# New places for the work of the first attention layer in a four-layer kernel on one core

## The chip, the core and the metric

The kernel runs on one core of a Trainium2 chip. Its time is device microseconds from start to end of the program, and the number shown is the median of several runs. The core has five engines that run side by side, each with its own queue of instructions: TensorE (PE, with its weight loads listed as PEld), VectorE (DVE), ScalarE (ACT), GpSimd (POOL) and SyncE (SP, which issues nearly all of the DMAs here).

## What is computed

The input x is 2048 x 640 in float32. Four layers follow each other, an attention layer A and a Fourier layer B in turn, each with a residual connection and a layer norm ahead of it:

```python
x = x + _A_ref(_layernorm(x), A_wqkv, A_wo)
x = x + _B_ref(_layernorm(x), dft_seq_re, dft_seq_im, dft_hid_re, dft_hid_im)
x = x + _A_ref(_layernorm(x), A_wqkv, A_wo)
x = x + _B_ref(_layernorm(x), dft_seq_re, dft_seq_im, dft_hid_re, dft_hid_im)
```

Layer A has 32 heads of 20 elements. Each position attends to 8 positions only: itself and those 2, 4, ... 14 places before it. So queries, keys and values come from one matrix product (640 x 1920), and so does the output (640 x 640), but the logits and the weighted sum of the values are elementwise products and sums over short windows:

```python
logits = einsum("bhsd,bhswd->bhsw", q, kg) * scale   # kg: 8 keys for each position
attn = softmax(where(mask, logits, -1e9))
o = einsum("bhsw,bhswd->bhsd", attn, vg)
```

Layer B is Real(DFT over the sequence of DFT over the hidden dimension): two products with 640 x 640 matrices and two with 2048 x 2048 matrices, of which symmetry leaves a part to be computed.

## The kernel before

**Precision.** Every matrix operand is split into a high part (a rounding copy, mostly by ACT) and a low part (the original less the high part, a subtract by DVE or POOL), and each product is three matmul passes: high x high, high x low, low x high. The subtract is called a low part below. It is made by `split` (L137, for weights `wq_split`), `wo_lo` (L584, output weights), `ln_lo` (L918, the normalised output of the layer), `c_lo` (L972, sequence matrix) and `pre_lo` (L956, the part of the sequence matrix that is split early and stored to DRAM as c0b). The high parts are `wo_hi` (L581), `c_hi` (L944) and `pre_hi` (L952).

**Attention.** The sequence is cut into 4 chunks (c) of 512 positions, the columns into 4 groups (q) of 480. 64 QKV groups of 15 matmuls each (`qkv_mm`, L369) write a bank; ACT copies it out (`qkv_evac`, L376); after every second group two DMAs store keys with values (kvb) and queries (qb) to DRAM (L385, L386). Windows of keys and values come back by DMA (`w_load`, L424), queries by `q_load` (L408) and a copy to PSUM by ACT (`q_copy`, L411).

The elementwise work has 32 units u of two halves each, 64 halves in all. For a half, DVE multiplies queries with windows of keys (`qk_mul`, L438, 128 x 1280 elements); POOL adds the upper ten elements of each head to the lower ten (L441); DVE sums the remaining ten (`qk_red`, L448). For the halves listed in `WHOLE` POOL's add is left out, and DVE sums all twenty. The softmax of a unit follows on DVE (L463 to L473) with the exponential on ACT (L456); then DVE multiplies with the values (`av_mul`, L478), and POOL adds the eight products in a tree of three adds (`av_tree`, L497, L498, L499). For the very last half DVE does this sum (L494). Then PE transposes the sums (`pc_pe`, L334, L342), and `wo_mm` (L522) multiplies with the output weights; DVE adds the residual (`wo_add`, L166), statistics and the norm of the next layer follow (`wo_stats`, `wo_fin`, `ln_hi` L914, `ln_lo` L918).

**The next layer's first product inside this one.** The sequence product of layer B (`z_mm`, L985) starts before the attention layer is done: 16 row blocks z, each in three thirds of five 128x512 matmuls, accumulating over z in five banks. Blocks 0 to 9 take a matrix that was split ahead (`pre_load` L948, `pre_hi`, `pre_lo`, `pre_store` L959; fetched by `c_get`), blocks 10 to 12 are loaded and split in place (`c_load`, `c_hi`, `c_lo`), the rest after the attention's end. Block z needs the normalised rows (c, j) with 4c + j = z, high and low part.

**What sets the order.** All of it is written out by hand. `at(step, phase, function, ...)` enters a call into a plan; the steps run from -7 to 66, in each the phases come in the order of `PHASES` (L851 and after), and the calls are emitted in that order inside a manual schedule. Each engine runs its instructions in the order emitted, and waits where data or a buffer isn't ready. Half s = 2u + jp of the elementwise work stands at step s (product), s + 1 (sum), s + 3 (values and tree). QKV group g stands at the step in `LEAD0` for the first 16 groups and then at one group a step, two at the even steps in `TWICE`. SP issues DMAs in this order too; a store stands right behind the instruction that makes its data, and all behind it in SP's queue wait with it.

A rest of the layer follows the last step: the last two rows of chunk 3 (transposes, output projection, norm) and blocks 13 to 15 of the sequence product.

## Time and profile before

| | us |
|---|---|
| median of 3 runs | 1759.59 |
| lowest, highest | 1754.35, 1760.87 |
| the profiled execution | 1757.63 |
| its span in the trace | 1755.8 |
| first attention layer in it, to the release of PE by POOL's last tree | 369.96 |

The profile is one execution. Its slices divide the span into 40 parts of 43.9 us, and a digit is the busy share in tenths. A row of a window view gives a stretch, its length, and for PE, PEld, DVE, ACT and POOL the busy time with the count of instructions; then the granted clock of PE, the DMA share and GB/s. A row of the timeline gives start and duration in microseconds, engine, line, operation, output and inputs by the program's names, shapes and count; a bracket at its end is the idle time of the engine before it, and what ended that. A row of the chain of waits gives start, duration, and what was worked on by the chain that ended last.

### The profile page before, as it was taken

To read this page: it belongs to the slowest core of one execution; us is meant where nothing else is said; L and a number is where in the kernel's file an instruction comes from. 1 tells how busy PE (TensorE), PEld (TensorE's weight loads), DVE (VectorE), ACT (ScalarE), POOL (GpSimd) and SP (SyncE) were. 2 spreads that over 40 slices of the span, in tenths; PEclk is the share of its full clock that TensorE was granted. 3 is DMA by queue.
4 is the path that set the end of the run, shared out by engine and by line. 5 is a ranking of instruction groups with operands and counts; after the bars stand their busy time and mean duration, and the time that the engine had idled before them with its cause. 6 is when DMAs were issued, how large, how long until landed. Compare 5 with 4: busy or idle time off the path is not lost.

```text
span 1755.8 us, 26454 instructions
## 1 busy us (share of the span) xinstructions
PE 1725.6 (98%) x8798; PEld 1501.8 (86%) x8798; DVE 1374.0 (78%) x2131; ACT 805.0 (46%) x1682; POOL 621.2 (35%) x585
## 2 busy tenths in 40 slices
PE   9999999989999999999999999999999999999999
PEld 7889897878888888888898899988788888888888
DVE  6999999988667767767648999989777677676673
ACT  4664544554444445445534434444434443443441
POOL 4799998940000000000028998889200000000000
PEclk9999999999999999999999999999999999999999
DMA  8996769859787787787657866798597868767861
GB/s 286 304 329 206 230 197 333 269 175 303 258 265 245 239 263 238 234 276 225 195 178 238 266 207 211 221 327 277 197 318 251 260 206 265 249 214 235 261 206 53
DMA packets 273961, 426.20 MB, mean 243 GB/s; under 512 B 22656, under 2 KB 153728, under 8 KB 273568
## 3 DMA queue, kind: packets, MB, share of 16 engines
q1 hardware_dynamic: 270624, 422.54, 73.8%
q10 hardware_dynamic: 3200, 1.97, 0.4%
q8 instruction: 70, 1.15, 0.3%
q14 instruction: 67, 0.55, 0.1%
HBM read 339.28 MB, written 85.14 MB: 242 GB/s over the span
## 4 chain that ended last, share of the span: by engine, by line
PE 75%; DVE 11%; DMA 7%; POOL 3%; issue 3%; ACT 1%; SPq 0%; DVEq 0%; ACTq 0%; POOLq 0%
PE m L369 21%; PE aux L1067 13%; PE t L1164 10%; PE m L1164 9%; PE pq L1164 5%; PE xt L1164 5%; PE aux L522 4%; DMA win<-cs_in 3%; PE m L985 2%; PE t L985 2%; DVE pr L478 2%; DVE pr L438 1%; PE xt L985 1%; POOL pr L497 1%; DMA win<-kvb 1%
## 5 line engine op out<-in xcount | busy, mean ns | idle before, releaser
L369 PE MATMUL m<-r,s 128*128 128x480 f32 x1920 | 435.8, 381 | 1.2 <-DVE r L649 0.5
L369 PEld LDWEIGHTS m<-r,s 128*128 128x128 f32 x1920 | 355.1, 188 | 54.9 <-DVE r L652 1.0
L1067 PE MATMUL aux<-r2a,zo 128*128 128x320 f32 x768 | 226.1, 309 | 0.0
L1157 ACT CAST r<-win 128x512 fp32r<-128x512 f32 x246 | 149.6, 620 | 163.6 <-DVE win L1193 90.1
L497 POOL TENSOR_TENSOR pr<-pr 128x640 f32<-128x640 f32 x126 | 205.3, 1629 | 32.6 <-DVE pr L478 32.1
L1067 PE MATMUL aux<-pr,zo 128*128 128x320 f32 x704 | 207.8, 309 | 0.0
L181 POOL TENSOR_TENSOR stats<-stats,mhalf 128x1 f32<-128x1 f32 (+1 forms) x40 | 30.0, 750 | 492.7 <-ACT stats L177 483.7
L438 DVE TENSOR_TENSOR pr<-pq,win 128x1280 f32<-128x1280 f32 x128 | 189.7, 1483 | 11.9 <-DMA win<-kvb 6.6
L1158 DVE TENSOR_TENSOR r<-win,r 128x512 fp32r<-128x512 f32 x246 | 165.4, 687 | 42.8 <-ACT r L1157 41.6
L478 DVE TENSOR_TENSOR pr<-pq,win 128x1280 f32<-128x1280 f32 x128 | 190.7, 1491 | 5.1
L441 POOL TENSOR_TENSOR pr<-pr 128x640 f32<-128x640 f32 x116 | 166.4, 1434 | 17.0 <-DVE pr L438 14.1
L1164 PE MATMUL m<-r,r 128*128 128x512 f32 x594 | 151.0, 389 | 0.0
L1067 PEld LDWEIGHTS aux<-r2a,zo 128*128 128x128 f32 x768 | 144.1, 188 | 1.9
L1164 PE MATMUL t<-r,r 128*128 128x512 f32 x498 | 133.8, 390 | 1.0 <-DVE r L1158 1.0
L1067 PEld LDWEIGHTS aux<-pr,zo 128*128 128x128 f32 x704 | 132.2, 188 | 2.1
L1164 PEld LDWEIGHTS m<-r,r 128*128 128x128 f32 x594 | 111.3, 188 | 22.9
L985 PE MATMUL m<-s,r 128*128 128x512 f32 x384 | 119.5, 399 | 7.5 <-DMA s<-c0b 3.4
L448 DVE TENSOR_REDUCE lg<-pr 128x64 f32<-128x640 f32 (+1 forms) x128 | 112.1, 876 | 8.8 <-POOL pr L441 8.3
L985 PE MATMUL t<-s,r 128*128 128x512 f32 x384 | 117.8, 394 | 0.2 <-DVE ot L1042 0.2
L498 POOL TENSOR_TENSOR pr<-pr 128x320 f32<-128x320 f32 x126 | 112.0, 889 | 9.9
L1164 PEld LDWEIGHTS t<-r,r 128*128 128x128 f32 x498 | 93.4, 188 | 21.4 <-DVE r L1158 1.4
L376 ACT COPY stg<-m 128x480 f32<-128x480 f32 x128 | 70.8, 554 | 81.7 <-PE m L369 61.5
(299 smaller groups left out, 3200.1 us busy)
## 6 DMA issues: line engine op xcount, KB each, us to landing
win<-cs_in SPq DMA_DIRECT2D x351, 256.0 KB, 3.8
r<-xc SPq DMA_DIRECT2D x240, 256.0 KB, 4.3
win<-kvb SPq DMA_DIRECT2D x96, 440.0 KB, 4.3
xa<-cs_in SPq DMA_DIRECT2D x121, 256.0 KB, 3.8
win<-kvb SPq DMA_DIRECT2D x64, 360.0 KB, 4.7
kvb<-stg SPq DMA_DIRECT2D x60, 320.0 KB, 5.3
xc<-stg SPq DMA_DIRECT2D x32, 512.0 KB, 4.2
s<-c0b SPq DMA_DIRECT2D x26, 512.0 KB, 6.2
```

Source lines behind the costliest of these rows:

```text
L369: nc.tensor.matmul(mt[g][:, : 3 * F], st[:, a, k], wq[q][:, b, k], start=n == 0, stop=n == 14)
L438: nc.vector.tensor_tensor(pr, q, wview(u, jp, 0, [[1, FE]]), op=ALU.mult)
L441: nc.gpsimd.tensor_tensor(pv[:, :, 0:10], pv[:, :, 0:10], pv[:, :, 10:20], op=ALU.add)
L448: nc.vector.tensor_reduce(lgs[u][:, :, 2 * jp : 2 * jp + 2].rearrange("p h j w -> p (j w) h"), prq.pop((u, jp)), axis=AX.X, op=ALU.add,)
L478: nc.vector.tensor_tensor(pr.rearrange("p j w (h d) -> p j w h d", d=DH), lgs[u][:, :, 2 * jp : 2 * jp + 2].rearrange("p h j w -> p j w h" ...
L497: g.tensor_tensor(pr[:, :, 0:4], pr[:, :, 0:4], pr[:, :, 4:8], op=ALU.add)
L498: g.tensor_tensor(pr[:, :, 0:2], pr[:, :, 0:2], pr[:, :, 2:4], op=ALU.add)
L985: self.last = nc.tensor.matmul(self.z[t][k], self.xn[c][:, a, j, k * P : (k + 1) * P], self.ct[s][:, b], start=s == 0 and i == 0, stop=s = ...
L1067: self.last = nc.tensor.matmul(self.ym[e][:, :320], zt[(k, a, ri)][:, j2 * P : (j2 + 1) * P], w[:, e * 320 : (e + 1) * 320], start=(k, a, ...
L1157: nc.scalar.copy(hi, raw)
L1158: nc.vector.tensor_tensor(lo, raw, hi.bitcast(F32), op=ALU.subtract)
L1164: nc.tensor.matmul(bank, w(a, kb), hl[b], start=start and (a, b) == (0, 0), stop=stop and (a, b) == (1, 0),)
```

## The change

Only the first attention layer's plan differs; the constants for the second one are written in another form and give the same plan.

- `LEAD0`: QKV groups 5 and 6 stand at step 0 instead of -2 and -1, together with group 7. Their order on PE is the same; their evictions on ACT and group 5's stores come later.
- `TWICE`: second groups at step 13 and 20 instead of 14 and 18.
- `WHOLE`: halves 45, 49, 51 and 59 get POOL's add back, halves 14, 39 and 52 lose it.
- `WQP`: weight low parts (1,2), (2,2) and (3,4) go from DVE to POOL, (2,3) and (3,1) from POOL to DVE.
- `PRD`, `PRV`, `PRP`: of the early split of the sequence matrix, the high parts of blocks 2 and 3 go from DVE to ACT and that of block 7 from ACT to DVE; the low part of block 1 goes to POOL; most stores come one step earlier, low part 2 comes to step 1, low part 3 to step 3.
- `WOR`, `WOS`, `WOP`: output weights are loaded at steps 10, 11 and 14, split at 11 to 17, and low parts 1 and 4 go from DVE to POOL.
- `LNV`: normalised low parts (1,2) and (2,0) go from POOL to DVE, (3,1) from DVE to POOL, behind the last tree.
- `ZT`: each third of the sequence product has a step and a phase of its own. Block 0 and two thirds of block 1 stand at 49, block 2 ahead of the transposes of step 52, two thirds of block 4 at 54, the rest of 4 and two of 5 at 55, block 8 mostly at 60, block 9 at 61 and 62, block 12 at 64. The loads, high and low parts of blocks 4 to 12 move with them; c_lo(10) stands at 61, c_lo(12) at 63.
- `W3`: the output projections of rows (3,0) and (3,1) stand at 61 and 63 instead of 60 and 61, with what follows them.

```diff
@@ -35,22 +35,19 @@
 NE = 8
 FE = 80
 HE = 4
-LEAD0 = (-7, -6, -5, -4, -3, -2, -1, 0, 1, 1, 2, 3, 3, 4, 5, 5)
+LEAD0 = (-7, -6, -5, -4, -3, 0, 0, 0, 1, 1, 2, 3, 3, 4, 5, 5)
 
 
 QJ1 = ((0, 0), (1, 0), (2, 0), (0, 1), (1, 1), (3, 0), (2, 1), (3, 1))
-TWICE = ((8, 10, 12, 14, 16, 18), (10, 14, 18, 20))
+TWICE = ((8, 10, 12, 13, 16, 20), (10, 14, 18, 20))
 OUTP = (((20, 24, 28, 32), (36, 40, 44, 46)), ((20, 24, 28, 32), (36, 40, 44, 46)))
 LNS = ((40, 52), (42, 52))
 
 
 LEAD2 = (-7, -6, -5, -4, -2, -1, 0, 0, 1, 1, 2, 3, 3, 4, 5, 5)
 WSTEP = (0, 0, 0, 1, 1, 2, 2, 3, 3, 4, 4, 5, 5, 6, 7)
-WHOLE = ((43, 45, 47, 49, 51, 55, 57, 59, 63), (51, 57, 63))
-ZTHIRDS = (
-    {49: 3, 50: 3, 51: 2, 52: 4, 56: 3, 57: 6, 58: 3, 59: 4, 60: 2, 61: 1, 62: 3, 63: 4, 64: 1},
-    {50: 3, 51: 5, 52: 1, 53: 1, 54: 1, 55: 1, 56: 5, 57: 4, 58: 3, 59: 3, 60: 1, 61: 1, 62: 4, 63: 2, 64: 4},
-)
+WHOLE = ((14, 39, 43, 47, 52, 55, 57, 63), (51, 57, 63))
+ZT = (((49, 'pe2'), (49, 'pe2'), (49, 'pe2'), (49, 'pe2'), (49, 'pe3w'), (50, 'pe3'), (51, 'pe'), (51, 'pe'), (51, 'pe'), (52, 'pe'), (52, 'pe'), (52, 'pe'), (54, 'pe3'), (54, 'pe3'), (55, 'pe3'), (55, 'pe3'), (55, 'pe3'), (56, 'pe3'), (57, 'pe3'), (58, 'pe3'), (58, 'pe3'), (58, 'pe3'), (59, 'pe3'), (59, 'pe3'), (60, 'peL'), (60, 'pe3'), (60, 'pe3'), (61, 'pe3'), (61, 'pe3'), (62, 'pe3'), (62, 'pe3'), (62, 'pe3'), (62, 'pe3'), (62, 'pe3'), (63, 'pe3'), (64, 'pe3'), (64, 'pe3'), (64, 'pe3'), (64, 'pe3')),
...
 TA = 65
 NWARM = 18
 STG = (-1, "dma2")
@@ -59,9 +56,19 @@
 NT = 8
 NP = 8
 NPAIR = 3
+CLO = (11, 12)
+WQP = (((0, 1), (0, 2), (0, 4), (1, 1), (1, 2), (1, 3), (2, 1), (2, 2), (3, 3), (3, 4)), ((0, 1), (0, 3), (1, 1), (1, 3), (2, 1), (2, 3), (3, 1), (3, 3)))
+LNV = (((1, 2), (2, 0), (2, 1), (2, 3), (3, 0), (3, 2), (3, 3)), ((3, 0), (3, 1), (3, 2), (3, 3), (2, 0), (2, 1), (2, 2), (2, 3), (0, 0), (0, 2)))
+PRD = ((3, 3, 3), (1, 2, 2), (1, 1, 1), (2, 3, 3), (1, 2, 2), (1, 2, 2), (1, 2, 2), (1, 2, 3), (1, 2, 2), (1, 2, 3))
+PRV = (0, 1, 7)
+PRP = (1,)
+WOP = (1, 4)
+WOS = (11, 13, 14, 16, 17)
+WOR = (10, 11, 14)
+W2 = ((52, 53, 54, 55), (52, 53, 54, 55))
+W3 = ((61, 63), (60, 61))
 KEEP = ((10, 11), (12, 13), (14, 15))
-PRE = {4: ("zo2", 0), 5: ("zo3", 2), 6: ("ot", 3), 7: ("zo2", 5), 8: ("zo3", 7), 9: ("ot", 8)}
-PRE.update({0: ('zo0', -5), 1: ('zo1', -4), 2: ('zo0', 0), 3: ('zo1', 0)})
+PRE = {4: ('zo2', 0), 5: ('zo3', 2), 6: ('ot', 3), 7: ('zo2', 5), 8: ('zo3', 7), 9: ('ot', 8), 0: ('zo0', -5), 1: ('zo1', -4), 2: ('zo0', 0), 3: ('zo1', 0)}
 XC = {
     5: ((0, 0), (2, 0), 1),
     7: ((2, 0), (2, 1), -1),
@@ -562,7 +569,7 @@
                     wq[(q, k)] = raw[:, k - k0]
 
         def wq_split(q, k):
-            split(wq[q][:, 0, k], wq[q][:, 1, k], wq[(q, k)], eng=nc.gpsimd if k % 2 else None)
+            split(wq[q][:, 0, k], wq[q][:, 1, k], wq[(q, k)], eng=nc.gpsimd if (q, k) in WQP[ly] else None)
 
         def wq_late(q, k):
             if k == 0:
@@ -581,7 +588,7 @@
             nc.scalar.copy(wo_s["w"][:, 0, k], wo_s[k // 2][:, k % 2])
 
         def wo_lo(k):
-            nc.vector.tensor_tensor(
+            (nc.gpsimd if k in WOP else nc.vector).tensor_tensor(
                 wo_s["w"][:, 1, k], wo_s[k // 2][:, k % 2], wo_s["w"][:, 0, k].bitcast(F32), op=ALU.subtract
             )
             nc.sync.dma_start(wob[:, :, k], wo_s["w"][:, :, k].bitcast(F32))
@@ -697,11 +704,11 @@
         sm = pq[:, o + NJ * HE : o + 2 * NJ * HE].rearrange("p (h j) -> p h j", j=NJ)
         mk = pq[:, o + 2 * NJ * HE : o + 2 * NJ * HE + SLOTS]
         for i in range(3 if first else 0):
-            at(10 + 2 * i, "dma", wo_raw, i)
+            at(WOR[i], "dma", wo_raw, i)
         for k in range(KD):
             if first:
-                at(12 + 2 * (k // 2) + k % 2, "actl", wo_hi, k)
-                at(13 + 2 * (k // 2) + k % 2, "misc", wo_lo, k)
+                at(WOS[k], "actl", wo_hi, k)
+                at(WOS[k] + 1, "misc", wo_lo, k)
             else:
                 at(8 + 2 * k, "dmas", wo_get, k)
 
@@ -790,8 +797,8 @@
                 at(t, "actl", handoff.ln_hi, c, j, nstats)
                 at(t + 1, "misc", handoff.ln_lo, c, j)
         for c, w, xtags in (
-            (2, (52, 53, 54, 55), None),
-            (3, (60, 61), ("xa", "xa")),
+            (2, W2[ly], None),
+            (3, W3[ly], ("xa", "xa")),
         ):
             for j in range(NJ):
                 if c == 2:
@@ -825,11 +832,11 @@
                 at(j2 - 3, "pe3", prev.ymm, NT - 1, j2, 0, KD)
                 at(j2 - 2, "actl", prev.yout, NT - 1, j2, stats)
         last = 66
-        thirds = [t for t, n in ZTHIRDS[ly].items() for _ in range(n)]
+        thirds = [t for t, _ in ZT[ly]]
         for z, (tag, t) in PRE.items() if first else ():
-            d = (2, 2, 3) if z < NJ else (1, 2, 3)
+            d = PRD[z]
             at(t, "dma", handoff.pre_load, z, tag)
-            at(t + d[0], "misc" if z < NJ else "actl", handoff.pre_hi, z)
+            at(t + d[0], "misc" if z in PRV else "actl", handoff.pre_hi, z)
             at(t + d[1], "misc", handoff.pre_lo, z)
             at(t + d[2], "dmac", handoff.pre_store, z)
         for z in range(len(thirds) // 3):
@@ -839,11 +846,11 @@
             elif first:
                 at(t - 2, "dmac", handoff.c_load, z)
                 at(t - 1, "hi", handoff.c_hi, z)
-                at(t - 1, "misc", handoff.c_lo, z, z in (11, 12))
+                at(t - 1, "misc", handoff.c_lo, z, z in CLO)
             else:
                 at(min(t - 1, 48 + z) if z < 3 else t - 1, "dmac", handoff.c_get, z)
             for p in range(3):
-                at(thirds[3 * z + p], "pe" if first and thirds[3 * z + p] == 52 else "pe2" if thirds[3 * z + p] == 52 else "pe3", handoff.z_mm, z, p)
+                at(*ZT[ly][3 * z + p], handoff.z_mm, z, p)
         if first:
             at(62, "dmac", handoff.c_load, 13)
             at(63, "hi", handoff.c_hi, 13)
@@ -914,7 +921,7 @@
             nc.scalar.copy(self.xn[c][:, 0, j], self.xl[(c, j)])
 
         def ln_lo(self, c, j):
-            on_vector = c == NC - 1 or c == 2 and (j % 2 or self.li == 3) or self.li == 3 and c == 0 and j % 2 == 0
+            on_vector = (c, j) in LNV[self.li // 2]
             (nc.vector if on_vector else nc.gpsimd).tensor_tensor(
                 self.xn[c][:, 1, j], self.xl[(c, j)], self.xn[c][:, 0, j].bitcast(F32), op=ALU.subtract
             )
@@ -948,12 +955,12 @@
             nc.sync.dma_start(self.raw[s][:, 1], cs[0][:, s, :])
 
         def pre_hi(self, s):
-            copy = nc.vector.tensor_copy if s < NJ else nc.scalar.copy
+            copy = nc.vector.tensor_copy if s in PRV else nc.scalar.copy
             copy(self.raw[s][:, 0].bitcast(F32R), self.raw[s][:, 1])
 
         def pre_lo(self, s):
             hi, lo = self.raw[s][:, 0], self.raw[s][:, 1]
-            nc.vector.tensor_tensor(lo.bitcast(F32R), lo, hi, op=ALU.subtract)
+            (nc.gpsimd if s in PRP else nc.vector).tensor_tensor(lo.bitcast(F32R), lo, hi, op=ALU.subtract)
 
         def pre_store(self, s):
             nc.sync.dma_start(c0b[:, s], self.raw.pop(s))
```

1 line of the change is left out of this document (added).

## Prediction

> **What bounds the kernel now.** I read the page from its top: busy shares, then the 40 slices, then the shares of the chain that ended last.
>
> ```profile
> span 1755.8 us, 26454 instructions
> PE 1725.6 (98%) x8798; PEld 1501.8 (86%) x8798; DVE 1374.0 (78%) x2131; ACT 805.0 (46%) x1682; POOL 621.2 (35%) x585
> ...
> DVE  6999999988667767767648999989777677676673
> ...
> POOL 4799998940000000000028998889200000000000
> ```
>
> TensorE (PE) is busy for 98% of the span, and the change takes no matmul away. So all that can be won is idle time of PE, in the one stage that is edited: the first attention layer, slices 0 to 8, where VectorE (DVE) and GpSimd (POOL) are full as well. I cut that layer at the places where PE starts and stops waiting. The columns are the stretch, its length, and busy time of PE, weight load, DVE, ACT and POOL.
>
> ```profile
> 0.00:54.00 54.00, 51.67 (x233) 40.60 (x234) 36.77 (x73) 27.12 (x57) 20.94 (x28) 1.00 0.83 281
> 54.00:74.00 20.00, 19.32 (x97) 16.15 (x96) 18.16 (x27) 12.90 (x31) 18.18 (x18) 1.00 1.02 348
> 74.00:270.00 196.00, 196.00 (x1024) 174.35 (x1023) 187.80 (x266) 105.53 (x265) 185.41 (x173) 1.00 0.78 244
> 270.00:316.00 46.00, 41.31 (x238) 36.42 (x237) 44.03 (x69) 20.79 (x55) 40.58 (x39) 1.00 0.98 343
> 316.00:370.00 54.00, 48.75 (x239) 40.42 (x237) 52.24 (x69) 26.08 (x62) 49.85 (x46) 0.97 0.70 228
> 370.00:389.00 19.00, 18.54 (x92) 16.10 (x92) 11.73 (x25) 12.15 (x28) 1.10 (x2) 0.91 0.47 160
> ```
>
> From 74 to 270 us (steps 8 to 47) PE has no gap: nothing that DVE or POOL does there can shorten it. From 270 to 370 PE idles 46.00 - 41.31 + 54.00 - 48.75 = 9.9 us, while DVE idles 3.7 us of the 100. There DVE and POOL set the pace and PE waits. The chain of waits at the end of the layer says which of the two.
>
> ```profile
> 346.34 1.50 DVE pr L478
> ...
> 347.91 1.59 POOL pr L497
> ...
> 366.83 1.54 POOL pr L497
> ...
> 369.38 0.54 POOL zo L499
> 369.96 0.89 PE pq L334 x4
> ```
>
> Up to 347.8 us DVE's value product L478 releases POOL; from 347.91 POOL runs its trees, adds and low parts without a gap, and PE transposes the last tree's sum at 369.96. I call this T. After T the stretch 370 to 389 is PE's own again (18.54 of 19.00). So the kernel gets shorter by as much as T comes earlier, if PE's own queue is not late at T. At most that is the 9.9 us plus the 0.7 us of 54 to 74.
>
> **The change part by part.** The terms are the start, DVE's work in the middle, DVE's work after 270, and POOL's and PE's places.
>
> *Start.* The first query product waits for a window, and the window's load stands in SyncE's queue behind a store of the pre-split sequence matrix (c0b) and a load that needs its place.
>
> ```profile
> 33.27 4.54 DMA c0b<-zo
> 37.83 0.33 SPq L948
> 38.21 4.92 DMA win<-kvb
> 43.22 1.49 DVE pr L438
> ```
>
> With QKV group 5 moved from step -2 to step 0 its two stores no longer stand ahead of the c0b store, and that store is itself moved to step -2. I estimate that the window is loaded some 2 us earlier. DVE also loses two copies of 0.43 us (L952, rows below) at step 2, and gets one at step 6; two pre-split subtracts go to steps 1 and 3, and one to POOL at step -2. DVE is therefore about 1.4 us earlier at step 4. But PE is nearly full there, and what it can give back is its idle time of 54 to 74, 20.00 - 19.32 = 0.7 us. I count **-0.7**. Against it: groups 5, 6 and 7 are still in the same order on PE, but group 7 writes the bank that group 5's eviction frees, and that eviction now stands on ACT behind the first query copy (L411) and four high-part casts of weights. The trace has no such wait; the nearest rows are that copy (0.44 us) and a window's landing (4.92 us), so the place is worth 0 to +4.9. I take 0: the copy is the row of the very operation, and a landing counts only if the query's load is late too. The upper end goes into the range.
>
> *Middle (74 to 270).* The durations by line and shape (count | busy, mean ns | idle before, releaser):
>
> ```profile
> L448 DVE TENSOR_REDUCE lg<-pr 128x64 f32<-128x640 f32 x55 | 44.7, 813 | 5.5 <-POOL pr L441 5.2
> L448 DVE TENSOR_REDUCE lg<-pr 128x64 f32<-128x1280 f32 x9 | 13.3, 1480 | 0.0
> L584 DVE TENSOR_TENSOR r2a<-zo,r2a 128x640 fp32r<-128x640 f32 x4 | 4.8, 1192 | 0.0
> L584 DVE TENSOR_TENSOR r2a<-ot,r2a 128x640 fp32r<-128x640 f32 x1 | 0.8, 812 | 0.0
> L952 DVE CAST zo<-zo 128x512 fp32r<-128x512 f32 x4 | 1.7, 424 | 1.0 <-DMA zo<-cs_in 0.9
> L918 DVE TENSOR_TENSOR r<-xa,r 128x640 fp32r<-128x640 f32 x2 | 1.7, 832 | 0.0
> L441 POOL TENSOR_TENSOR pr<-pr 128x640 f32<-128x640 f32 x55 | 78.9, 1435 | 8.1 <-DVE pr L438 5.3 <-DMA zo<-cs_in 2.6
> L918 POOL TENSOR_TENSOR r<-r,r 128x640 fp32r<-128x640 f32 x6 | 9.4, 1569 | 0.0
> ```
>
> A half that DVE sums whole costs DVE 1.48 - 0.81 = 0.67 us more and spares POOL an add of 1.43. Here halves 14 and 39 become whole: DVE +1.34, POOL -2.9. Two of the five output-weight subtracts (wo_lo, L584) go to POOL, one of the first four and the last (from tile ot): DVE -1.19 - 0.81 = -2.0, POOL +2 x 1.57 = +3.1 (L918 on POOL, the same width). Net: DVE -0.7, POOL +0.2. PE hides it while it lasts, but at 270 DVE takes over, and then it is 0.7 us further on: **-0.7**. The moved output-weight loads and casts, and the weight subtracts exchanged between the two engines (one more on POOL, 0.65 us off DVE), fall into ACT's and POOL's slack of this time; 0.
>
> *After 270.* Halves 45, 49, 51 and 59 go back to POOL and 52 becomes whole: DVE -3 x 0.67 = -2.0, POOL +3 x 1.43 = +4.3. Two normalised low parts, (1,2) and (2,0), come to DVE: +1.66; (3,1), 0.83, leaves it, for POOL after its last tree. DVE: -2.0 + 0.8 = **-1.2**. Is there room on POOL? Its waits for DVE, in order:
>
> ```profile
> 260.31 1.58 POOL L497 TENSOR_TENSOR pr<-pr 128x640 f32<-128x640 f32 x1 [1.22 <-DVE pr L478]
> 280.43 1.58 POOL L497 TENSOR_TENSOR pr<-pr 128x640 f32<-128x640 f32 x1 [1.35 <-DVE pr L478]
> 290.71 1.57 POOL L497 TENSOR_TENSOR pr<-pr 128x640 f32<-128x640 f32 x1 [2.02 <-DVE pr L478]
> 347.91 1.58 POOL L497 TENSOR_TENSOR pr<-pr 128x640 f32<-128x640 f32 x1 [2.34 <-DVE pr L478]
> ```
>
> The four waits, 6.9 us, stand just behind the halves that get their adds back (45, 49, 51, 59), and four adds are 5.7 us. So they are hidden, with 1.2 us left, to which two low parts of 1.57 us that POOL loses come. If that cover is gone, each add costs up to 1.43.
>
> A DVE subtract of two arrays can meet a running POOL instruction. Then both are longer:
>
> ```profile
> 338.64 2.04 DVE L918 TENSOR_TENSOR r<-r,r 128x640 fp32r<-128x640 f32 x1
> 340.60 2.06 DVE L972 TENSOR_TENSOR s<-stg,s 128x512 fp32r<-128x512 f32 x1
> ...
> 339.94 2.17 POOL L497 TENSOR_TENSOR pr<-pr 128x640 f32<-128x640 f32 x1
> ```
>
> 2.04 against 0.83 on DVE, and 2.17 against 1.58 on POOL. The two added low parts may each meet one: 0 to +1.2 each. The split of c_lo(10), now one step after its neighbour, may meet one less: 0 to -1.2. I let these cancel.
>
> [...]
>
> *PE's places.* The sequence product's thirds (L985), the last output projections (L522) and their loads move by one to five steps. Three rows of PE from the end of the layer:
>
> ```profile
> 359.18 0.73 PE L985 MATMUL m<-s,r 128*128 128x512 f32 x2 [2.03 <-POOL s L972]
> 369.96 0.88 PE L334 MATMUL pq<-ident,zo 128*128 128x128 f32 x4 [1.81 <-POOL zo L499]
> ...
> 378.62 0.63 PE L985 MATMUL m<-s,r 128*128 128x512 f32 x2
> ```
>
> PE waits 1.81 us for T; so PE's places cost nothing as long as they are no later by that much, and gain nothing, for T waits on POOL. A split c_lo(12) one step later is followed by its thirds, one step later too. If they fill no gap, PE comes late at T by what is lost: the 2.03 us of the first row again, less the 1.81, about +0.2. The low part (3,1), put on POOL behind the last tree, ends at T + 1.6; the product that reads it cannot start before 378.62, T + 8.7. Loads and stores moved with these steps keep their order of need on SyncE's queue.
>
> **Sum**: -0.7 - 0.7 - 1.2 = -2.6 us. The profiled execution took 1757.63 us (span 1755.8, and 1.8 around it), which makes 1755.0; that execution is 2.0 below the median of the runs shown (1759.59; 1754.35 to 1760.87). Against the median the forecast is **1757.0**.
>
> **The rivals.**
>
> *Fuller gain.* DVE's waits for POOL's adds and others within the layer go too: 5.2 us for L441 (row of L448 above, 8 waits), part of them at the halves 14 and 39 themselves. With 4.3 of them saved: -6.9, **1752.7**. For it: POOL is relieved at steps 14 and 39, and half 39 has the longest of them.
>
> ```profile
> 231.33 0.82 DVE L448 TENSOR_REDUCE lg<-pr 128x64 f32<-128x640 f32 x1 [1.08 <-POOL pr L441]
> ```
>
> Against it: between them POOL gets the two wo_lo, and PE is full until 270.
>
> *No gain.* PE's 196.00 us without a gap also sets when DVE gets its data, since query copies stand behind PE's evictions on ACT, and what is won after 270 is given back where PE comes late (c_lo(12), low part (3,0), each a step later): 0, **1759.6**.
>
> *Moving to POOL helps nothing.* DVE's low parts of wo, moved to POOL, stretch what they meet there: the -2.0 goes, and +1.34 of the middle stays, so -0.7 + 1.3 - 1.2 = -0.6, **1759.0**. For it: the lengthened rows at 338 to 342. Against: the first four L584 were lengthened where they were (mean 1.19 against the last one's 0.81), and a POOL subtract is no DVE instruction that meets anything.
> [...]
>
> *Slower: POOL becomes the bound before 347.9.* Place: POOL's queue between the low part of wo at step 18 and half 59. It gets 3.1 (wo_lo) + 4 x 1.43, loses 3 x 1.43 and two low parts (3.1): +1.4. If each of the two added DVE low parts meets a POOL instruction, 2 x 0.6 on POOL and 2 x 1.2 on DVE come on top: +5.0, and none of DVE's savings counts: **1764.6**. It decides from the point where adds and stretches at 45 to 59 exceed the 6.9 us of waits: 5.7 + 1.2 is just that. Against it: POOL has two low parts less from 316 on.
>
> **How the numbers follow.** About 0.5% (8.8 us) is what a measurement of this kernel tells from no change. Chances: the forecast 0.44, fuller gain 0.16, no gain 0.10, moving helps nothing 0.08, POOL the bound 0.22. The fuller gain stands at -6.9; with the start's 1.4 instead of 0.7, a relieved meeting (1.2) and the weight subtract (0.65) it passes -8.8, for 0.11 of its 0.16. POOL's rival stands at +5.0, and passes +8.8 with the late group 7 (+4.9) on top: 0.13 of its 0.22. So faster 0.11, same 0.76, slower 0.13. The range reaches from the fuller gain, 1752.7 less 3.7 (these three terms, 2.55, and one more meeting of 1.2), to POOL's rival with a little of group 7: 1749 to 1766.
>
> **What would show it.** In the changed profile: the first query product at about 41 us instead of 43.2; PE without a gap from 74 to 270, and the same length of that stretch; the wait of 1.08 at half 39 gone; POOL's waits for L478 behind halves 45, 49, 51 and 59 under 1 us; DVE's busy time between 270 and T about 1.2 us less; T 2 to 3 us earlier, with PE waiting there; 19 us from T to the layer's end. I am wrong if DVE waits for POOL between 120 and 350 us for more than the 5.2 us now (then POOL is the bound), if PE does not wait at T (then PE's places are), if T moves and the end does not, or if the three later layers, which the change leaves alone, move by more than 1 us.

## The result, and the profile after

The changed kernel takes 1750.51 us (median of 20 runs, 1747.03 to 1757.43) against 1755.93 us of the kernel before in the same session (20 runs, 1751.63 to 1761.02): ratio 0.9969, interval 0.9957 to 0.9981, which is 3.3 to 7.6 us less. The forecast was 2.6 us less, 1757.0 us with a range of 1749 to 1766. Sign and range were right; the forecast's size, 2.6 us, is smaller than the interval's lower end. Of the 6.5 us between 1757.0 and 1750.51, 3.7 come from the base: the forecast stood on the 1759.59 us of three runs of the kernel before, and twenty give 1755.93.

The profiled execution took 1755.72 us. Its page, and the windows with the cuts of before (stretch, length, busy time of PE, weight load, DVE, ACT, POOL, then PE's clock):

```profile
span 1753.9 us, 26453 instructions
...
PE 1724.9 (98%) x8798; PEld 1502.2 (86%) x8798; DVE 1372.8 (78%) x2127; ACT 804.9 (46%) x1683; POOL 627.9 (36%) x589
```

```profile
0.00:54.00 54.00, 52.21 (x233) 40.74 (x234) 37.33 (x70) 28.98 (x61) 26.77 (x32) 1.00 0.85 295
54.00:74.00 20.00, 20.00 (x102) 17.43 (x101) 19.52 (x26) 12.73 (x31) 16.91 (x16) 1.00 0.97 328
74.00:270.00 196.00, 194.83 (x1014) 172.63 (x1013) 186.98 (x266) 104.45 (x262) 185.53 (x174) 1.00 0.77 243
270.00:316.00 46.00, 41.73 (x232) 37.00 (x231) 41.65 (x66) 20.55 (x55) 40.82 (x39) 0.96 0.93 333
316.00:370.00 54.00, 49.51 (x251) 42.03 (x249) 51.75 (x72) 26.73 (x64) 50.90 (x47) 0.97 0.69 229
370.00:389.00 19.00, 18.36 (x94) 15.74 (x94) 13.92 (x28) 13.38 (x31) 1.42 (x3) 1.00 0.63 217
```

PE's 0.7 us of idle time at 54 to 74 is gone. In the middle, which had none, there are now 1.2 us of it: waits of 0.43 us at 80.05, 0.20 at 132.86 and 0.54 at 141.88. In this execution DVE has 2.9 us less to do from 270 to 370 (93.4 against 96.3); in a second one of the same kernel it is 96.8, so that this figure doesn't carry. At the end of the layer the timeline of the changed kernel (line numbers are 7 higher there: L506 is the last add of the tree, L341 the transposes, L529 the output projection, L992 the sequence product) reads:

```profile
366.45 2.90 PE L529 MATMUL aux<-r2a,zo 128*128 128x320 f32 x18 [0.19 <-ACT zo L364]
369.19 0.60 PE L341 MATMUL pq<-ident,zo 128*128 128x128 f32 x4
...
377.06 0.63 PE L992 MATMUL m<-s,r 128*128 128x512 f32 x2
...
368.21 0.54 POOL L506 TENSOR_TENSOR zo<-pr 128x160 f32<-128x160 f32 x1
```

POOL's last tree ends at 368.75 instead of 369.91, and PE, which waited 1.81 us for it before, comes to the transposes just behind it and waits for nothing. The product goes on at 377.06 instead of 378.62. So this execution wins 1.6 us in the first layer, and 1.9 at the end of the span. The remainder of the measured 3.3 to 7.6 us isn't in these two traces; the experiments come back to it.

### The profile page after: what moved, and what is told of

It is laid out like the page before. It is cut to its first block, busy times and chain, and to the rows that moved or that the text cites. A ratio compares the mean times of both kernels' runs of the same rounds, so it can differ in the third digit from the quotient of the medians.

```text
span 1753.9 us, 26453 instructions
## 1 busy us (share of the span) xinstructions
PE 1724.9 (98%) x8798; PEld 1502.2 (86%) x8798; DVE 1372.8 (78%) x2127; ACT 804.9 (46%) x1683; POOL 627.9 (36%) x589
## 4 chain that ended last, share of the span: by engine, by line
PE 72%; DVE 11%; DMA 8%; POOL 4%; issue 3%; ACT 1%; SPq 0%; DVEq 0%; ACTq 0%; POOLq 0%
PE m L376 17%; PE aux L1074 14%; PE t L1171 10%; PE m L1171 10%; PE pq L1171 5%; PE xt L1171 5%; PE aux L529 5%; PE m L992 2%; DMA win<-kvb 2%; PE t L992 2%; DVE pr L445 2%; DVE pr L485 2%; DMA xc<-stg 1%; POOL pr L504 1%; DMA win<-cs_in 1%
## 5 line engine op out<-in xcount | busy, mean ns | idle before, releaser
L504 POOL TENSOR_TENSOR pr<-pr 128x640 f32<-128x640 f32 x126 | 207.0, 1643 | 33.9 <-DVE pr L485 33.8
L448 POOL TENSOR_TENSOR pr<-pr 128x640 f32<-128x640 f32 x117 | 168.5, 1440 | 14.7 <-DVE pr L445 11.8
L992 PE MATMUL m<-s,r 128*128 128x512 f32 x384 | 120.1, 400 | 8.3 <-DMA s<-c0b 5.5
L992 PE MATMUL t<-s,r 128*128 128x512 f32 x384 | 118.1, 396 | 0.2 <-DVE ot L1049 0.2
L383 ACT COPY stg<-m 128x480 f32<-128x480 f32 x128 | 71.0, 555 | 84.4 <-PE m L376 63.4
```

Of the source, the lines that this page charges most:

```text
L448: nc.gpsimd.tensor_tensor(pv[:, :, 0:10], pv[:, :, 0:10], pv[:, :, 10:20], op=ALU.add)
L504: g.tensor_tensor(pr[:, :, 0:4], pr[:, :, 0:4], pr[:, :, 4:8], op=ALU.add)
L992: self.last = nc.tensor.matmul(self.z[t][k], self.xn[c][:, a, j, k * P : (k + 1) * P], self.ct[s][:, b], start=s == 0 and i == 0, stop=s = ...
```

## The experiments

Kernels whose parts are undone use the changed file with the constants of before, which gives each engine the same instructions in the same order as the kernel before. The same readings serve all: POOL's last tree (its end, T), the start of PE's 500th and 1900th matmul, counted from 0 in each trace (the 1900th lies in the rest of the layer, at 386.12 us before), and the stretch from the start of DVE's product of half 46 (261.54 us before) to the end of the last tree. That stretch holds the late part of the change but for its first edit, at half 45, and leaves out what a kernel won or lost ahead of it.

| kernel | 500th, against before | half 46 to last tree | last tree ends | 1900th starts | whole time, ratio to before (interval) |
|---|---|---|---|---|---|
| before | 0 | 108.37 | 369.91 | 386.12 | |
| before_again | -0.51 | 108.43 | 369.79 | 386.11 | |
| changed | -0.83 | 107.60 | 368.75 | 384.56 | 0.9969 (0.9957 to 0.9981) |
| again | -0.08 | 105.84 | 367.95 | 383.71 | 0.9966 (0.9945 to 0.9987) |
| p_start | -1.37 | 108.35 | 368.98 | 384.38 | 0.9976 (0.9959 to 0.9993) |
| s_lead | -0.80 | 108.34 | 369.05 | 384.43 | |
| p_mid | +0.95 | 108.39 | 371.67 | 387.06 | 1.0000 (0.9983 to 1.0018) |
| p_late | +1.17 | 106.07 | 368.60 | 384.43 | 0.9983 (0.9968 to 0.9998) |
| l_pe | +0.32 | 107.75 | 369.88 | 385.75 | |
| l_dve | +0.47 | 108.71 | 370.40 | 385.48 | |
| u_wo4 | -1.48 | 110.35 | 370.72 | 386.58 | |
| u_cget | +0.07 | 106.39 | 368.14 | 383.89 | 0.9982 (0.9967 to 0.9996) |
| best2 | -0.42 | 108.68 | 369.98 | 385.73 | 0.9977 (0.9964 to 0.9990) |
| best3 | -1.07 | 105.19 | 366.30 | 382.05 | 0.9973 (0.9961 to 0.9986) |

**How far one trace can be trusted.**

before_again is the kernel before without an edit.

> The kernel before once more, for a second profile. Theory 1 (the first layer repeats, the later layers scatter): PE leaves the first layer (its 1900th matmul) within 0.8 us of the first profile's 386.1 us, the waits of 1.66 us at 275 and of 0.73 at 137 are there again, and the end differs by up to some 8 us for reasons after 500 us. Theory 2 (the first layer itself scatters by several us, so that its -1.6 to -2.4 us in the profiles is chance): 2 us or more off at the 1900th matmul.

Its single run took 1754.9 us. The first layer repeats: last tree and 1900th matmul within 0.12 us, though the 500th came 0.51 us earlier. The two spans differ by 2.8 us (1755.8 and 1753.0), all of it after the layer. Theory 1 holds for this pair: the wait of 0.73 us at 137 is there again (0.75). The 1.66 us at 275 stand in neither timeline as one wait; PE waits 0.43 us at 275.86 in the first and 0.83 at 271.83 in the second.

again is the changed kernel without an edit.

> The changed kernel once more, for a second profile and a ratio of its own. The first profile of it took 1755.7 us, 5.2 above the median of its 20 runs, and shows PE waiting 2.74 us for block 3 of the sequence matrix (DMA, at 291.7 us) with slow matmuls behind it. Theory 1 (an odd landing in that execution): the new profile takes 1748 to 1751 us, that wait is under 1 us, and the layer's end comes 3 to 5 us earlier than in the first. Theory 2 (the wait belongs to the kernel): the wait is again 2 us or more and the layer ends within 1 us of the first profile's; the 5 us lie in later layers. Ratio to before 0.996 to 0.998 by both.

It took 1753.89 us (median), 1756.1 in its profile. Theory 1 is right on the wait and wrong on its price: the wait for block 3 is 0.32 us instead of 2.74, as the two timelines show (the first three rows are the changed kernel's first profile, the last is this one), but the layer's end comes only 0.85 us earlier, and the span is no shorter.

```profile
291.71 0.73 PE L992 MATMUL m<-s,r 128*128 128x512 f32 x2 [2.74 <-DMA s<-c0b]
...
295.17 1.49 DVE L445 TENSOR_TENSOR pr<-pq,win 128x1280 f32<-128x1280 f32 x1 [1.56 <-DMA win<-kvb]
302.68 0.49 DVE L173 SCALAR_TENSOR_TENSOR r<-aux,r 128x320 f32<-128x320 f32 x1 [1.70 <-PE aux L529]
```

```profile
290.30 0.74 PE L992 MATMUL m<-s,r 128*128 128x512 f32 x2 [0.32 <-DMA s<-c0b]
```

From the 1900th matmul to the last, where all fourteen traces run the same instructions in the same order, they take between 1360.7 us (u_cget) and 1373.5 us (p_mid). This scatter, 12.8 us wide, is larger than the whole effect. A single trace tells nothing of the whole time.

Of the first layer it tells less than the pair above suggests. The start of before is also in p_mid, p_late, l_pe and l_dve, and the 500th matmul of these six lies between -0.51 and +1.17 us; in the eight traces with the changed start it lies between -1.48 and +0.07. The means are +0.40 and -0.75. The stretch from half 46 to the last tree repeats far better: the five traces in which the late part is as before take 108.34 to 108.43 us.

**The three parts, each alone.**

p_start:

```diff
+LEAD0 = (-7, -6, -5, -4, -3, 0, 0, 0, 1, 1, 2, 3, 3, 4, 5, 5)
+PRD, PRV, PRP, WQP   # as in the change
```

> The kernel before with the start alone: QKV groups 5 and 6 at step 0, the exchanged weight low parts, the early split of the sequence matrix. The forecast's step: -0.7 us, PE 0.7 to 1.0 us ahead by step 10 and still so at 270 us, ratio 0.9996. Rival (the lead is lost, because something after 74 us holds both kernels, as in the changed kernel, where PE was 0.9 ahead at 130 us and 0.3 behind at 150): PE level with before at 270 us, ratio 1.000. Rival (the start carries most of the measured gain): ratio 0.998.

Median 1756.66 us. PE is 1.37 us ahead at its 500th matmul and 1.19 at 262 us; the tree ends 0.9 us and the 1900th matmul starts 1.7 us earlier. At the tree that is little more than the forecast's 0.7, and the lead isn't lost here; the other 0.8 us arise behind the tree (see s_lead). The interval (-1.2 to -7.2 us) holds the last rival's 0.998, and the forecast's 0.9996 lies just outside it.

p_mid:

```diff
+TWICE = ((8, 10, 12, 13, 16, 20), ...)
+WHOLE = ((14, 39, 43, 45, 47, 49, 51, 55, 57, 59, 63), ...)
+WOP, WOS, WOR   # as in the change
```

> The kernel before with the middle alone: halves 14 and 39 whole, output-weight splits moved and two low parts on POOL, second QKV groups at 13 and 20. The forecast's step: -0.7 us at the end, nothing at 270 us on PE, ratio 0.9996. Rival (POOL becomes the bound at step 18): DVE waits about 2 us for POOL's add at about 137 us instead of 0.73, PE is 0.5 to 1.3 us behind before from 150 to 270 us, ratio 1.0003 to 1.0007.

Median 1759.46 us. The interval holds both ratios; the trace has it with the rival. DVE's wait at half 19, first here and then in p_start, where the middle is as before:

```profile
138.50 0.82 DVE L455 TENSOR_REDUCE lg<-pr 128x64 f32<-128x640 f32 x1 [1.98 <-POOL pr L448]
```

```profile
135.26 0.82 DVE L455 TENSOR_REDUCE lg<-pr 128x64 f32<-128x640 f32 x1 [0.70 <-POOL pr L448]
```

PE falls back by 1.2 us between its 600th and 700th matmul (+0.89 to +2.06 against before) and stays there. The last tree ends 1.76 us later than before's. This trace was 0.95 us late at the 500th matmul already, ahead of its first edit in the elementwise work; the other 0.8 us are what the middle part costs, give or take some 0.4: in before_again, s_lead and p_start the tree lies -0.1 to +0.4 us off what their 500th matmul says. At the 1900th matmul only 0.94 us of all this is left, since from the tree to there before takes 16.21 us and this trace 15.39; s_lead, below, shows where that comes from.

p_late:

```diff
+WHOLE = ((43, 47, 52, 55, 57, 63), ...)
+LNV, ZT, W3   # as in the change
```

> The kernel before with the late part alone: halves 45, 49, 51, 59 back to POOL and 52 whole, normalised low parts exchanged, new places of the sequence product's thirds and of the last two output projections. The forecast's step: -1.2 us, ratio 0.9993, T set by POOL's last tree with PE waiting. Rival (the thirds' places are the gain: PE's idle time of 270 to 370 us is filled and PE no longer waits at T): -3 to -5 us, ratio 0.997 to 0.998, PE waits under 0.5 us at T.

Median 1755.79 us. Despite a start that was 1.17 us late, the tree ends 1.3 us and the 1900th matmul starts 1.7 us earlier; from half 46 to the tree it takes 2.3 us less than before, twice the forecast's 1.2. PE no longer waits at T, as the rival had it; of its 3 to 5 us the layer's end shows 1.7. Its time, -0.4 to -5.6 us, allows either.

**What in the start.** s_lead:

```diff
-LEAD0 = (-7, -6, -5, -4, -3, -2, -1, 0, 1, 1, 2, 3, 3, 4, 5, 5)
+LEAD0 = (-7, -6, -5, -4, -3, 0, 0, 0, 1, 1, 2, 3, 3, 4, 5, 5)
```

> The kernel before with QKV groups 5 and 6 at step 0, and nothing else. Theory 1 (the stores of group 5 leaving SyncE's queue make the start faster, as the forecast said): the window's load for the first unit's second half is issued 1 to 2.5 us earlier than at 38.2, PE is 0.5 to 1.0 us ahead at its 400th matmul. Theory 2 (what the start won, 1.4 us, came from DVE's split copies and subtracts going elsewhere): PE within 0.3 us of the kernel before at its 400th matmul.

One run, 1751.16 us. The window's load is issued at 35.6 us instead of 38.2, and PE is 0.80 us ahead at its 400th matmul: theory 1. Tree and layer's end are those of p_start (369.05 and 368.98, 384.43 and 384.38): the place of the groups makes the gain of the start that is seen there, and the moved splits of the sequence matrix none. p_start's larger lead at the 500th matmul, by 0.57 us, is within what the start scatters.

The tree ends 0.9 us earlier in both, the 1900th matmul starts 1.7 earlier. The other 0.8 us come from PE's clock behind the tree. The rows of 371 to 374 us, before and in s_lead (the clock is the third column from the right):

```profile
371.00:374.00 3.00, 2.70 (x11) 2.71 (x12) 1.80 (x5) 0.52 (x2) 0.00 (x0) 0.56 0.00 0
```

```profile
371.00:374.00 3.00, 2.91 (x20) 2.75 (x19) 1.53 (x6) 0.70 (x3) 0.00 (x0) 1.00 0.00 0
```

Both traces of the kernel before run at half clock there (0.56 and 0.50), none of the other twelve does (1.00 in each). In the four others with before's places on PE (p_start, s_lead, p_mid, l_dve) the slow matmuls come ahead of the tree's end, at some 364 to 371 us: 18 matmuls of the output projection take 4.34, 4.44, 4.44 and 4.07 us there, against 2.90 in before (the clock is 0.58 at 368 to 371 in p_mid), where PE would wait for the tree anyway. From the tree to the 1900th matmul these four take 15.1 to 15.4 us, the two of before 16.2 and 16.3, the eight with the new places 15.8 to 15.9. p_mid has the start of before, so the start doesn't decide this; what does is not shown. The query products of s_lead, and under them what held DVE in the changed kernel:

```profile
41.37 1.49 DVE L445 TENSOR_TENSOR pr<-pq,win 128x1280 f32<-128x1280 f32 x1 [0.84 <-ACT pq L418]
48.15 1.49 DVE L445 TENSOR_TENSOR pr<-pq,win 128x1280 f32<-128x1280 f32 x1
53.36 1.48 DVE L445 TENSOR_TENSOR pr<-pq,win 128x1280 f32<-128x1280 f32 x1
```

```profile
41.51 0.69 DVE L963 TENSOR_TENSOR zo<-zo 128x512 fp32r<-128x512 f32 x1 [2.51 <-ACT zo L959]
...
53.63 1.49 DVE L445 TENSOR_TENSOR pr<-pq,win 128x1280 f32<-128x1280 f32 x1 [1.31 <-DMA win<-kvb]
```

In the changed kernel a low part of the split (L963), now at step 1, stands ahead of the query product on DVE and waits 2.51 us for its high part on ACT; the product follows at 42.85. DVE makes that up at the next product (46.37, against 48.15 in s_lead and 49.45 before) and loses it again at the one after, which waits 1.31 us for its window and starts at 53.63 (53.36 in s_lead, 54.65 before).

**What in the late part.** l_pe has the places on PE alone, l_dve the elementwise work alone:

```diff
+ZT, W3   # l_pe: as in the change; WHOLE and LNV as before
```

> The kernel before with the new places of the sequence product's thirds and of the last two output projections alone; DVE's and POOL's work is as before but for its order. Theory 1 (the late gain is DVE's shorter work, T lies on POOL's last tree): POOL's last tree ends within 0.4 us of 369.9, and the layer's end within 0.6 us of before. Theory 2 (the gain is PE's, which no longer waits behind T): the layer's end 1 to 1.7 us earlier, PE without a wait at the transposes after the last tree. The late part as a whole gave -1.7 us at the 1900th matmul, with 0.5 us of later start.

```diff
+WHOLE = ((43, 47, 52, 55, 57, 63), ...)   # l_dve
+LNV   # as in the change; ZT and W3 as before
```

> The kernel before with the late part's elementwise changes alone: halves 45, 49, 51, 59 back to POOL, 52 whole, normalised low parts exchanged. The forecast's step of -1.2 us, taken by itself. Theory 1 (DVE's shorter work makes the late gain): POOL's last tree 1.0 to 1.8 us earlier than before's (369.9), DVE waits less, POOL's waits for L485 behind 45, 49, 51 and 59 under 1 us. Theory 2 (the low parts and the new places of the product only work together): the tree within 0.5 us of before's.

One run each: 1757.42 and 1755.59 us. Alone, PE's places leave the tree where it was (369.88) and give 0.4 us at the 1900th matmul: theory 1 of that pair. Alone, DVE's shorter work leaves the tree where it was as well (370.40, with a start 0.5 us late): theory 2. The 0.6 us that it shows at the 1900th matmul lie behind the tree, where before has its half clock. On the stretch from half 46 to the tree l_pe wins 0.6 us and l_dve loses 0.3; both together (p_late) win 2.3. DVE's own account, from the product of half 46 to the value product of half 63: before it is busy for 102.1 us and waits 4.0; in l_dve 100.2 and 5.3; in p_late 100.5 and 2.8. What l_dve saves on DVE goes into new waits, at the residual add of the output projections:

```profile
317.93 0.49 DVE L173 SCALAR_TENSOR_TENSOR r<-aux,r 128x320 f32<-128x320 f32 x1 [0.56 <-PE aux L529]
...
343.92 0.49 DVE L173 SCALAR_TENSOR_TENSOR xa<-aux,xa 128x320 f32<-128x320 f32 x1 [0.79 <-PE aux L529]
350.61 0.49 DVE L173 SCALAR_TENSOR_TENSOR xa<-aux,xa 128x320 f32<-128x320 f32 x1 [0.71 <-PE aux L529]
```

Making DVE shorter hands the bound to PE there. With the new places on PE too (p_late, and again, the second profile of the changed kernel) none of these waits is over 0.3 us. Whether the thirds' places or the projections' at 61 and 63 take them away was not tried apart; the first of the three waits lies well ahead of those two projections.

**What in the middle.** u_wo4:

```diff
-WOP = (1, 4)
+WOP = (1,)
```

> The changed kernel with the low part of wo's last block back on DVE (it stood on POOL at step 18). Theory 1 (this one instruction is POOL's bound in the middle): DVE's wait of 2.01 us for POOL's add at 137 us is again about 0.7, PE's lag of 1.2 us from 150 us on is gone, POOL's last tree ends 0.5 to 1.2 us earlier than in the changed kernel's profiles (368.8 and 368.0), and the layer's end moves less, since PE stands without a gap ahead of it. Theory 2 (the lag is made by the second QKV group at steps 13 and 20, or by whole halves): the lag stays, and DVE gets 0.8 us longer.

One run, 1758.94 us. The wait at half 19 is gone entirely, so this one subtract on POOL (1.57 us at 133.79 in the changed kernel, just ahead of half 19's add) makes it. But PE's lag between the 600th and 700th matmul is 1.0 us still. Where it arises can be read off the changed kernel:

```profile
132.86 0.66 PE L341 MATMUL xt<-ident,xa 128*128 128x128 f32 x4 [0.20 <-ACT xa L205]
...
141.88 1.34 PE L376 MATMUL m<-r,s 128*128 128x480 f32 x5 [0.54 <-ACT stg L383]
...
141.07 0.31 ACT L463 ACTIVATE lg<-lg 128x128 f32<-128x128 f32 x1 [4.05 <-DVE lg L474]
```

At 132.86 the transposes wait for a norm on ACT (L205): the second QKV group, which stood ahead of them at step 18, is at step 20 now. Counted from start to start this costs 0.35 us. At 141.88 a QKV group waits for an eviction on ACT (L383), which stands behind an exponential (L463) that waited for DVE, and DVE had its 2.01 us wait for POOL ahead of that; this costs 0.7 us. In u_wo4 the first wait is there again and the second is gone. In its place the transposes at 136.76 and what follows them lose 0.6 us: they come right behind their casts on ACT, and ACT had waited 3.15 us for DVE, which has its subtract back (1.26 us at 129.46). So with the group at step 20 the subtract delays PE through ACT on whichever of the two engines it stands, and a third of the lag comes from the group's place. That place was not tried by itself. And the layer's end is later, not earlier (386.58): this execution had the late landing at 291 us (2.60 us of waiting on PE, 1.42 and 1.70 on DVE) and a half-clock stretch (0.50 at 338 to 341) behind a wait of 3.66 us at 337. What the subtract costs at the end stays open.

**Three attempts at a better version.** u_cget fetches block 4 of the sequence matrix a step later; best2 puts block 8 into PE's gap at step 60; best3 does both:

```diff
-max(thirds[3 * z - 7] + 1, t - 3)
+max(thirds[3 * z - 7] + 1, t - 3) + (z == 4)   # u_cget, best3
```

```diff
-(60, 'peL'), (60, 'pe3'), (60, 'pe3'), (61, 'pe3')
+(60, 'pe'), (60, 'pe'), (60, 'pe'), (61, 'pe3')   # best2, best3: block 8
```

> The changed kernel with the fetch of block 4 of the sequence matrix one step later (52 instead of 51). In the first profile of the changed kernel it was issued at 288.0 us, just behind two window loads, which then took 7.8 us to land, and PE waited 2.74 us for block 3 and DVE 1.56 us for a window. Theory 1 (that fetch takes the bandwidth that the window loads need): the window loads at 287 us land in 6 us or less, DVE waits under 0.5 us for a window between 290 and 300, the layer ends 1 to 2 us earlier than in that profile (384.6 us at PE's 1900th matmul). Theory 2 (chance: in the second profile the same loads took 5.9): no difference to the second profile (383.7).

> The changed kernel with block 8 of the sequence product ahead of the second transposes of step 60, where PE waited 2.0 to 3.9 us for ACT's cast (at 336 us) and ran at half clock behind it in three of four profiles. Theory 1 (PE's late places are the bound at T in the changed kernel): the wait at 336 us falls under 1 us, no half clock from 336 to 343, PE waits at T for POOL's last tree again, the layer's end 0.3 to 1.5 us earlier. Theory 2 (POOL's last tree is the bound, PE only just behind it): T within 0.4 us of the changed kernel's, the layer's end no earlier. Ratio to before 0.995 to 0.998.

> Both of these: block 4 fetched at step 52, block 8 ahead of the second transposes of step 60. If each acts alone: 1 to 2.5 us before the changed kernel at the layer's end, ratio to before 0.994 to 0.998. If the two waits only change places: as the changed kernel.

Medians 1754.07, 1752.70 and 1752.65 us; all three intervals overlap with that of the changed kernel, so none is shown to be better. In the traces: u_cget's window load lands in 6.7 us, between theory 1's 6 and the 7.8 seen, DVE waits 0.39 us for its window, and the layer's end, 0.7 us ahead of the first profile, equals that of again: undecided between the landing's cause and chance. Of the four traces with both the start and the early fetch of block 4 (changed, again, u_wo4, best2) three have DVE wait over 1 us for that window, of the two with the later fetch neither (0.39 and 0.62); that is too few to call it shown.

best2 had the late landing too (2.43 us at block 3), so its end says little. Its gap does what was expected. Here are the wait at step 60 and the clock behind it (third column from the right), in u_cget, which has the gap, and in best2:

```profile
335.96 0.58 PE L349 MATMUL aux<-ot,nident 128*128 128x256 f32 x1 [3.68 <-ACT s L345]
...
335.00:338.00 3.00, 2.04 (x6) 1.75 (x7) 2.93 (x4) 0.90 (x3) 2.84 (x3) 0.59 0.53 149
338.00:341.00 3.00, 3.00 (x13) 2.43 (x12) 3.00 (x4) 0.85 (x3) 3.00 (x3) 0.84 0.95 336
```

```profile
337.83 0.38 PE L349 MATMUL aux<-ot,nident 128*128 128x256 f32 x1 [0.26 <-ACT s L345]
...
338.00:341.00 3.00, 2.23 (x15) 1.97 (x15) 2.93 (x5) 0.06 (x1) 2.84 (x4) 1.00 0.78 226
```

A wait of 1.33 us follows in best2 and 1.50 us for POOL's c_lo(12) later, so part of the gap only moved. In best3, with a smaller delay there (PE waits 1.78 us for block 3, DVE 0.62 for the window), the last tree ends at 366.30 and the 1900th matmul starts at 382.05, 1.7 us ahead of the better profile of the changed kernel (its 500th was 1.0 us ahead). That is the earliest layer end of all; its whole time (0.9973) shows no more than the others.

## Why the prediction was right, and where it failed

**Only PE's idle time in the first layer can be won, and at most some 10 us.** Right in the main: the layer's end moved by 1.6 and 2.4 us, and what the changed kernel won lies at the start and after 270. But 0.4 of it, in either trace, lies behind T, which the forecast took to be PE's own and fixed at 19 us: before has its half clock there (0.56 and 0.50 at 371 to 374).

**Start, -0.7.** Right in mechanism, and near in size: alone the start brings 0.9 us at the tree (s_lead, p_start). That it shows 1.7 at the 1900th matmul is due to the clock behind the tree, and not to the start. The product came at 41.37 us in s_lead, against the 41 of the forecast; in the changed kernel at 42.85, since a low part of the split now stands at step 1 ahead of it, and the forecast did not look when its high part on ACT is done. The bound of 0.7 us was somewhat low. It was read from busy rows, and a matmul's end as shown covers short gaps behind it (a 128x480 matmul is shown 378 ns long, and the next one starts 217 ns after its start): before's two gaps of 0.20 us at 55.01 and 0.48 at 73.38 cost 0.25 and 0.64, counted from start to start. That group 7 would wait for an eviction cost nothing that shows: PE has no gap there.

**Middle, -0.7.** Failed, in its sign too: p_mid's tree comes some 0.8 us later than its start explains. The step said that the two low parts of wo fall into POOL's room, since POOL gets only 0.2 us net. The sum is right, but the places aren't: half 14, which relieves POOL, lies ahead of step 18, where the second low part comes, and half 39 far behind it. DVE's wait of 0.73 us became 2.01, and through ACT it reached PE, which was to hide it; the low parts left on DVE met more of POOL's work (1.41 us each instead of 1.19: in the changed kernel all three start while an add of POOL's runs, and of the four in before one starts behind it and takes 0.81). The rival of POOL as the bound stood at this very place, with a price of 5.0 us; POOL was the bound for one instruction, for 1.3 us. The rival that moving to POOL helps nothing had the middle at +1.3, nearer to what came, but for stretched subtracts and not for this wait. What DVE wins at half 39, where the wait of 1.08 us is gone as forecast, doesn't outweigh it.

**After 270, -1.2, and PE's places, 0.** The term was sized at half, and PE's places were wrongly put at nothing. From half 46 to the tree the stretch is 2.3 us shorter in p_late and 2.5 in again. DVE's busy time, the forecast's 1.2, is 1.6 us less in both, nearly as said. The rest are DVE's waits, 4.0 us before and 2.8 and 2.6 there, which the forecast left as they were. They fall only with the places on PE: without them (l_dve) they rise to 5.3, and the tree doesn't move. "PE's places gain nothing, for T waits on POOL" was true of l_pe and wrong as a term: the places are what lets DVE's gain through.

How DVE's subtracts meet POOL's work, which the forecast let cancel, went both ways. Here are the kernel before, then again, by line and shape:

```profile
L972 DVE TENSOR_TENSOR s<-stg,s 128x512 fp32r<-128x512 f32 x2 | 3.8, 1904 | 0.0
L918 DVE TENSOR_TENSOR r<-r,r 128x640 fp32r<-128x640 f32 x2 | 3.4, 1692 | 0.0
```

```profile
L925 DVE TENSOR_TENSOR r<-r,r 128x640 fp32r<-128x640 f32 x4 | 5.5, 1364 | 0.0
L979 DVE TENSOR_TENSOR s<-stg,s 128x512 fp32r<-128x512 f32 x2 | 2.5, 1262 | 0.0
```

The splits of the sequence matrix lose 1.3 us in every trace with the new late part. The normalised low parts, two more of this shape, cost 2.1 us more in again, and 1.9 in p_late. In the first profile of the changed kernel they met less, and four cost 3.7 us (three of them 0.81 to 0.82 each, one 1.29); there DVE's busy time fell by 3.1 us, but a late window made it wait, and the stretch was only 0.8 us shorter.

The adds of halves 45 to 59 were hidden, as said: where POOL waited 6.9 us in four places, it waits 0.5 in the changed kernel. One of the four was misread. The wait at 347.91 stands behind the add of half 61; the add of half 59 is missing at 334, where POOL didn't wait.

**The sum, -2.6.** In the first layer it is near: -1.2 and -2.0 us at the tree, -1.6 and -2.4 at the layer's end. That is luck in part. The start gave -0.9, the middle +0.8 and the late part -2.3, where the forecast had -0.7, -0.7 and -1.2: an error of 1.5 us and one of 1.1 cancel.

In the whole time the kernel won 3.3 to 7.6 us, in the second series 2.3 to 9.7. The first interval excludes the layer's 1.6 to 2.4 us. Some of that difference is the scatter of the start: at the 500th matmul the two traces of before lie at -0.26 on average, the six with this start at +0.40; the two of the changed kernel at -0.46, the eight with that start at -0.75. If such a lead carries to the layer's end, the gain there is nearer 3 us than 2; that is an estimate from the table. That the later layers, whose instructions are the same, run faster behind this one isn't shown by any trace: they scatter by 12.8 us between traces and show no trend with the first layer's end. Whether the rest of the excess lies there stays open. The parts agree with their sum: 0.9976, 1.0000 and 0.9983 multiply to 0.9959.

**The clauses of the end.** "Wrong if PE does not wait at T (then PE's places are the bound)": that is so in the changed kernel, but by some 0.4 us only (the tree ends at 368.75, the transposes start at 369.19); T is nearly a tie. DVE waits for POOL between 120 and 350 us for 3.2 us in the changed kernel and 3.7 in again, which is under the 5.2 named; but 5.2 is the sum of the whole layer, and in that stretch before has 3.2. PE was to be without a gap from 74 to 270 and has 1.2 us of them; T was to come 2 to 3 us earlier with PE waiting, and came 1.2 and 2.0 earlier. On the three later layers, which were not to move by more than 1 us, the scatter allows no answer.

## What to carry to other kernels

Where three engines follow closely on each other, the gain of an edit is not a term of a sum: shorten one, and the saving turns into its waits for the next, until the others are given their room too (here PE's places alone won 0.6 us, DVE's shorter work alone lost 0.3, both together won 2.3); so test the parts together and apart. A balance of busy time over a stage doesn't place the relief: what is added to a full queue must be relieved ahead of that point, not on average (here POOL got 0.2 us net, and DVE's wait for it went from 0.73 to 2.01). And a moved instruction brings along what it waits for: before a subtract is put ahead in an engine's queue, look when its input is made (here it waited 2.51 us, and the query product stood behind it). Last, put a reading where the edit acts: a stretch that holds the edit and begins behind the scatter of the start repeats to 0.1 us here, while the end of the layer mixes in the start and the clock.

## What was not expected of the hardware

A short wait of PE was paid twice here. Behind its 1.93 us wait at T the second trace of before runs at half clock for three microseconds, and 12 matmuls that take 2.17 us in l_dve take 3.39:

```profile
369.85 0.66 PE L334 MATMUL pq<-ident,zo 128*128 128x128 f32 x4 [1.93 <-POOL zo L499]
370.99 3.39 PE L522 MATMUL aux<-r2a,zo 128*128 128x320 f32 x12 [0.48 <-ACT zo L338]
...
371.00:374.00 3.00, 3.00 (x11) 3.00 (x12) 1.70 (x5) 0.21 (x1) 0.00 (x0) 0.50 0.00 0
```

```profile
370.46 0.66 PE L341 MATMUL pq<-ident,zo 128*128 128x128 f32 x4 [1.74 <-POOL zo L506]
371.57 2.17 PE L529 MATMUL aux<-r2a,zo 128*128 128x320 f32 x12 [0.46 <-ACT zo L345]
```

The wait in l_dve is nearly as long (1.74 us), and the clock stays full (1.00 at 371 to 374); there the slow matmuls had come ahead of it already (18 of them take 4.07 us from 364.65). In p_mid a shorter wait (1.26 us at 365.00) is followed by half clock (0.58 at 368 to 371). So the length of one wait doesn't decide. In the stretch from 368 to 371 us PE worked for 0.67 of 3 us in the second trace of before, and for 1.26 in l_dve; whether that makes the difference is not shown. From the tree to the 1900th matmul the two traces with half clock behind it take 16.2 and 16.3 us, the four others with the same places on PE 15.1 to 15.4. Where the half clock falls is worth 0.8 to 1.2 us beyond the wait itself, which the forecast left out.
